# A scratch buffer of its own for each head's maximum in a fused attention and MLP kernel

## The chip, the cores and the metric

The kernel runs on one core of one Trainium2 chip. The metric is the device time of one execution in microseconds (us). Five engines work beside each other, each through its own instructions in order: TensorE (PE; its weight loads are shown as PEld), VectorE (DVE), ScalarE (ACT), GpSimd (POOL) and SyncE (SP), which here issues nearly all DMAs. They wait for each other through semaphores.

## The reference

With x of 2048 rows by 640 columns:

```python
def _A_ref(x, wqkv, wo):                 # H = 32 heads of Dh = 20, window W = 256
    q, k, v = ...                        # x @ wqkv, split into heads
    scores = einsum("bhqd,bhkd->bhqk", q, k) * Dh ** -0.5
    mask = (i - j >= 0) & (i - j < W)
    p = softmax(where(mask, scores, -1e9))
    o = einsum("bhqk,bhkd->bhqd", p, v)
    return o.reshape(B, S, D) @ wo

def _B_ref(x, w1, b1, w2, b2):           # 640 -> 1536 -> 640
    h = relu(x @ w1 + b1) ** 2
    return h @ w2 + b2

xn = layernorm(x)
return x + _A_ref(xn, ...) * silu(_B_ref(xn, ...))
```

All inputs and the output are float32.

## The kernel before

The 2048 rows are 16 blocks of 128. A product that has to be exact is made of three matmuls, with each factor cut into a high and a low part.

A first stage, up to about 113 us, normalizes x, transposes it, and makes v and the first group of q and k. The main stage then runs over steps. A step is one pair of heads (16 pairs) and one block of 128 queries (16 blocks), with some more steps behind, since the later parts of a step lag 13 and 15 steps. The order of every engine's instructions is written out by the program: `tc.manual_schedule` keeps it, and a planner (`due`, `fill`, `clock`) decides at build time how much filling work goes between the parts of a step. One step issues:

- `scores` (L642): for each of the two heads one matmul into a PSUM bank `sps`. Both banks come from the pool `pat`, tag `s`, with two buffers, so the next step's `sps` for the first head takes the bank that the first head's maximum has read, and likewise for the second.
- `scores_t` (L683), for the step 13 back: the transposed scores `stps` of both heads, into one buffer of two banks.
- every 8 steps `max_rows` (L660): the maxima gathered in `mt` are transposed into `stps`, negated, split and stored into two rows of q, so that `stps` comes out with the row's maximum taken off.
- `maxima` (L654): for each of the two heads one VectorE instruction that adds the mask to the scores of up to 384 keys, writes the sum to `junk`, and writes its maximum over the keys into one column of `mt`. Nothing reads `junk`. In the trace one such call is a reduction (CUSTOM_DVE_ANT_0) and the read of its accumulator into `mt` (DVE_READ_ACCUMULATOR2_ANT), both at L658.
- `exps` (L694): the exponential of `stps` into `p` on ScalarE, with two selections on GpSimd for the mask.
- filling work: q and k of the later heads (`qkps`), and the MLP's two products, `hps` (evacuated by ScalarE) and `yps`. `yps` is emptied by an addition on VectorE, `ysb` at L1185, and its bank is then reused. Each filling product is issued in two halves of 64 rows that TensorE works on side by side (L640).
- `values` (L724), once per 8 blocks: a burst of `ops` matmuls that multiplies p by v.

After the last step come the output product `wops` (L800) and its evacuation (L1381).

The weights of the MLP are cut into parts on the way: a copy on ScalarE and a subtraction on VectorE (L991).

A buffer of a pool is taken by its tag. When a tile is taken from a tag whose buffers are all in use, the first instruction that writes it waits until the last use of the tile that had the buffer before. For `junk`, with one buffer for both heads, that last use is the other head's maximum; as both are VectorE's, the wait is one for VectorE's own semaphore.

Of the kernel before, what the change touches and what calls it, by code (L numbers as in the profile page):

```python
# [11 lines left out]
BF16 = mybir.dt.bfloat16  # L12
# [3 lines left out]
P = 128  # L16
# [50 lines left out]
def attn_mlp_kernel(ctx: ExitStack, tc, x, wqkv, wo, w1, b1, w2, b2, out):  # L67
# [516 lines left out]
    at2 = ctx.enter_context(tc.tile_pool(name="at2", bufs=2))  # L584
# [68 lines left out]

    def maxima(p, q, ss, nk):  # L654
        for hh in range(2):
            junk = at2.tile([P, 3 * P], BF16, tag="junk", bufs=1, name="junk")
            m = MG * hh + q % MG
            nc.vector.tensor_tensor_reduce(out=junk[:, :nk], in0=ss[hh][:, :nk], in1=mask[:, 3 * P - nk:], scale=1.0, scalar=-3.0e38, op0=ALU.add, op1=ALU.max, accum_out=mts[q // MG % 2][:, m:m + 1])  # L658

# [756 lines left out]
    with tc.manual_schedule(engines={E_.PE, E_.Activation, E_.DVE, E_.Pool, E_.SP}):  # L1416
# [7 lines left out]
        for s in range(steps):  # L1424
# [29 lines left out]
            if a:  # L1454
                maxima(*a, *sc)
# [51 lines left out]
```

## Time and profile before

| | |
|---|---|
| time, median of 3 runs | 837.44 us (837.16 to 837.87) |
| the profiled execution's own time | 838.13 us |
| its span, first to last instruction | 836.4 us |
| PE busy | 826.2 us (99%) |
| PEld busy | 779.0 us (93%) |
| DVE busy | 477.8 us (57%) |
| ACT busy | 425.5 us (51%) |
| POOL busy | 364.2 us (44%) |
| TensorE's granted clock | 1.000 |

A row of a group reads: line, engine, operation, what it writes and reads with the shapes, how many, then busy time and the mean of one in ns, and the engine's idle time before them with what ended it. A row of the timeline reads: start and duration in us, engine, line, operation, count, and in square brackets how long the engine had been idle before and what released it. A row of the chain in order of time has start, duration and what ran; "issue" there is time in which nothing that the profile shows was waited for, and DVEq is an instruction of VectorE's sequencer, such as a semaphore wait. PE and PEld are two streams of one engine; a matmul's duration contains its way through the array, so that matmuls overlap.

### The profile page before, as it was taken

The page shows a single profiled execution, that of the slowest core. Times are in us where ns is not written, and L with a number is a line of the kernel's source. Part 1 is how long each engine was busy: PE and PEld are TensorE (multiplying, and loading weights), DVE is VectorE, ACT ScalarE, POOL GpSimd, SP SyncE. Part 2 cuts the span into 40 slices and gives each one's busy share as a digit, 9 for nine tenths or more (in the row PEclk, how much of TensorE's full clock was granted, in tenths as well). Part 3 has the DMA queues.
Part 4 walks back from the last instruction along what each step waited for, and adds up shares of the span by engine and source line. Part 5 has one row for each costly group of instructions (what it writes and reads, how often), then busy time and mean ns, then how long its engine had stood idle before and what let it go on. Part 6 is the DMA issues. An engine that isn't in the chain of part 4 may idle for free.

```text
span 836.4 us, 25137 instructions
## 1 busy us (share of the span) xinstructions
PE 826.2 (99%) x10082; PEld 779.0 (93%) x10082; DVE 477.8 (57%) x1398; ACT 425.5 (51%) x760; POOL 364.2 (44%) x672
## 2 busy tenths in 40 slices
PE   8999999999999999999999999999999999999997
PEld 8999999989889999999999989999999999999997
DVE  7855457656578455455455476655455455246763
ACT  6254323545566744744754754844644744664321
POOL 5177900334344542533542543643543643552442
PEclk9999999999999999999999999999999999999999
DMA  6999577878697555546083536585266557346962
GB/s 236 299 390 348 182 215 269 238 260 282 232 324 262 142 173 156 127 157 174 21 268 130 121 108 181 134 244 176 59 222 172 130 177 224 92 131 199 373 251 80
DMA packets 88812, 166.40 MB, mean 199 GB/s; under 512 B 10232, under 2 KB 36472, under 8 KB 87672
## 3 DMA queue, kind: packets, MB, share of 16 engines
q1 hardware_dynamic: 88536, 164.63, 62.7%
q8 instruction: 79, 1.29, 0.7%
q14 instruction: 37, 0.30, 0.1%
q10 hardware_dynamic: 160, 0.16, 0.1%
HBM read 93.66 MB, written 70.52 MB: 196 GB/s over the span
## 4 chain that ended last, share of the span: by engine, by line
PE 94%; DVE 2%; DMA 2%; issue 1%; ACT 1%; SPq 0%; POOL 0%; DVEq 0%; POOLq 0%; ACTq 0%
PE hps L640 20%; PE yps L640 20%; PE qkps L640 13%; PE ops L731 10%; PE wops L800 8%; PE stps L690 5%; PE sps L650 4%; PE vps L239 4%; PE qkps L214 3%; PE vps L362 3%; PE tps L181 1%; DVE junk L658 1%; DMA k_d<-slo 1%; DMA qs<-q_d 1%; PE vps L417 0%
## 5 line engine op out<-in xcount | busy, mean ns | idle before, releaser
L658 DVE CUSTOM_DVE_ANT_0 junk<-sps,mask 128x384 bf16<-128x384 f32 (+2 forms) x512 | 272.4, 532 | 250.9 <-PE sps L650 91.3
L696 ACT ACTIVATE p<-stps 128x768 f32<-128x768 f32 (+2 forms) x256 | 197.5, 772 | 255.5 <-PE stps L690 236.6
L697 POOL TENSOR_SCALAR_AFFINE_SELECT p<-p 128x256 f32<-128x256 f32 x256 | 109.8, 429 | 336.4 <-ACT p L696 334.0
L640 PE MATMUL yps<-w,hh 64*128 64x320 f32 x1536 | 226.1, 309 | 2.2 <-DVE ysb L1185 2.0
L640 PE MATMUL hps<-xb,w 64*128 64x256 f32 (+1 forms) x2100 | 210.0, 304 | 0.0
L640 PEld LDWEIGHTS hps<-xb,w 64*128 64x128 f32 x2100 | 194.7, 186 | 3.5 <-issue 2.7
L640 PEld LDWEIGHTS yps<-w,hh 64*128 64x128 f32 x1536 | 187.9, 185 | 7.3 <-DVE ysb L1185 4.4
L640 PE MATMUL yps<-w,hl 64*128 64x320 f32 x768 | 179.3, 308 | 0.0
L650 PE MATMUL sps<-ks,qs 60*128 60x384 f32 (+2 forms) x512 | 125.4, 335 | 1.0 <-DVE mt L658 1.0
L690 PE MATMUL stps<-qs,ks 62*128 62x384 f32 (+2 forms) x512 | 122.0, 334 | 0.1
L640 PEld LDWEIGHTS yps<-w,hl 64*128 64x128 f32 x768 | 121.4, 185 | 0.4 <-issue 0.4
L640 PE MATMUL qkps<-xT,wgqh 64*128 64x512 f32 x320 | 99.4, 391 | 0.0
L640 PE MATMUL qkps<-xT,wgkh 64*128 64x512 f32 x320 | 98.2, 391 | 0.0
L699 POOL TENSOR_SCALAR_AFFINE_SELECT p<-p 128x256 f32<-128x256 f32 x224 | 95.5, 426 | 0.0
L731 PE MATMUL ops<-p,vp 128*21 128x128 f32 (+1 forms) x2128 | 86.6, 311 | 0.0
L731 PEld LDWEIGHTS ops<-p,vp 128*21 128x21 f32 x2128 | 63.6, 101 | 21.2 <-issue 6.3
L650 PEld LDWEIGHTS sps<-ks,qs 60*128 60x128 f32 x512 | 78.4, 185 | 4.3 <-DVE mt L658 2.2
L690 PEld LDWEIGHTS stps<-qs,ks 62*128 62x128 f32 x512 | 77.5, 187 | 0.7 <-ACT p L696 0.6
L1155 POOL TENSOR_TENSOR hl<-sq,hh 128x512 fp32r<-128x512 f32 x48 | 62.1, 1293 | 16.1 <-ACT sq L1154 15.5
L800 PE MATMUL wops<-wo,oT 128*128 128x320 f32 (+2 forms) x384 | 62.0, 310 | 0.0
L640 PE MATMUL qkps<-xT,wgkl 64*128 64x512 f32 x160 | 61.4, 393 | 0.0
L640 PE MATMUL qkps<-xT,wgql 64*128 64x512 f32 x160 | 61.4, 390 | 0.0
(163 smaller groups left out, 1234.2 us busy)
## 6 DMA issues: line engine op xcount, KB each, us to landing
ks<-k_d SPq DMA_DIRECT2D x64, 240.0 KB
qs<-q_d SPq DMA_DIRECT2D x64, 240.0 KB
xb<-xs SPq DMA_DIRECT2D x60, 256.0 KB
k_d<-shm SPq DMA_DIRECT2D x20, 512.0 KB
q_d<-shm SPq DMA_DIRECT2D x20, 512.0 KB
xs<-xT SPq DMA_DIRECT2D x8, 1280.0 KB
y<-ysb SPq DMA_DIRECT2D x28, 320.0 KB
o<-osb SPq DMA_DIRECT2D x64, 128.0 KB
```

The source lines that it names most:

```text
L214: nc.tensor.matmul(ps, wt[:, c, :], xT[part][b][:, c * BT + t0:c * BT + t0 + n], start=m == 1, stop=m == 3 * KC)
L239: nc.tensor.matmul(ps, xT[xp][b][:, c * BT + t * P: c * BT + (t + 1) * P], wv[wp][:, c, nh * HALF:(nh + 1) * HALF], start=first and m == 0 ...
L640: return nc.tensor.matmul(out, a[r], b_[r], skip_group_check=True, **kw)
L650: nc.tensor.matmul(ss[hh][:, :nk], qs[i][o, q * P:(q + 1) * P], ks[i][o, k0 * P:k0 * P + nk], start=True, stop=True)
L658: nc.vector.tensor_tensor_reduce(out=junk[:, :nk], in0=ss[hh][:, :nk], in1=mask[:, 3 * P - nk:], scale=1.0, scalar=-3.0e38, op0=ALU.add, o ...
L690: nc.tensor.matmul(tps[:, hh, :n], ks[i][o, kb * P:(kb + 1) * P], qs[i][o, kb * P:kb * P + n], start=True, stop=True)
L696: nc.scalar.activation(p32[:, :, :n], tps[:, :, :n], AF.Exp, scale=SCALE)
L697: nc.gpsimd.affine_select(p32[:, :, 0:P], p32[:, :, 0:P], pattern=[[0, 2], [1, P]], compare_op=ALU.is_ge, fill=0.0, base=0, channel_multip ...
L699: nc.gpsimd.affine_select(p32[:, :, 2 * P:], p32[:, :, 2 * P:], pattern=[[0, 2], [-1, P]], compare_op=ALU.is_gt, fill=0.0, base=0, channel ...
L731: nc.tensor.matmul(ot[r0:r0 + VW, c0:c0 + len(part), :], vps[p][:, kb // 4, kb % 4, hh, :], pts[p, kb][:, hh, :].rearrange("p (t n) -> p t ...
L800: nc.tensor.matmul(ps, a, b_, start=j == 0, stop=j == n - 1)
L1155: nc.gpsimd.tensor_sub(hh[1][:, :BT], sq, f32(hh[0]))
```

## The change

`maxima` takes the scratch tile under a tag of its own for each of the two heads, `junk0` and `junk1`, with one buffer each. Everything else is as it was.

```diff
     def maxima(p, q, ss, nk):
         for hh in range(2):
-            junk = at2.tile([P, 3 * P], BF16, tag="junk", bufs=1, name="junk")
+            junk = at2.tile([P, 3 * P], BF16, tag=f"junk{hh}", bufs=1, name="junk")
             m = MG * hh + q % MG
             nc.vector.tensor_tensor_reduce(out=junk[:, :nk], in0=ss[hh][:, :nk], in1=mask[:, 3 * P - nk:], scale=1.0, scalar=-3.0e38, op0=ALU.add, op1=ALU.max, accum_out=mts[q // MG % 2][:, m:m + 1])
```

## The prediction

> **What bounds the kernel now.** I read the page's busy times first, then its chain, then the waits of TensorE's two streams, and then the maxima themselves, line L658, in the source view, the chain in order of time and the timeline.
>
> ```profile
> PE 826.2 (99%) x10082; PEld 779.0 (93%) x10082; DVE 477.8 (57%) x1398; ACT 425.5 (51%) x760; POOL 364.2 (44%) x672
> PE 94%; DVE 2%; DMA 2%; issue 1%; ACT 1%; SPq 0%; POOL 0%; DVEq 0%; POOLq 0%; ACTq 0%
> L658 DVE CUSTOM_DVE_ANT_0 junk<-sps,mask 128x384 bf16<-128x384 f32 (+2 forms) x512 | 272.4, 532 | 250.9 <-PE sps L650 91.3
> ```
>
> TensorE is the bound: busy for 826.2 of 836.4 us and 94% of the chain. VectorE, where the change is, works 57% of the span. A gain on VectorE alone is worth nothing; it counts only where TensorE stands still for VectorE. The waits views of PE and of its weight loads (PEld) name those places (total us, times, longest):
>
> ```profile
> PE yps L640 <- DVE ysb L1185: 2.0, 4, 1.0
> PE sps L650 <- DVE mt L658: 1.0, 2, 0.7
> PEld yps L640 <- DVE ysb L1185: 4.4, 9, 1.3
> PEld sps L650 <- DVE mt L658: 2.2, 5, 1.0
> ```
>
> They are two kinds. The scores matmul of L650 waits until a maximum has read its PSUM bank (mt is what the maximum's second instruction writes). A matmul into yps waits until the addition of L1185 has emptied its bank, and that addition often stands behind a pair of maxima in VectorE's queue. These views leave out waits under about 0.15 us.
>
> Now the pair. Source view of L658, and the chain in order of time at one pair:
>
> ```profile
> L658 DVEq EVENT_SEMAPHORE  x514: 21/21/358, 112.9 to 722.8; - x172
> L658 DVE DVE_READ_ACCUMULATOR2_ANT mt<- x512: 75/83/86, 113.7 to 723.4; 128x1 f32 x171
> ...
> 235.41 0.56 DVE junk L658
> 235.97 0.02 DVE mt L658
> 235.99 0.03 issue
> 236.01 0.02 DVEq L658
> 236.03 0.09 issue
> 236.12 0.11 DVE junk L658
> ```
>
> Each of the 512 maxima is three things: a semaphore wait of VectorE's own queue (x514), the reduction, and the read of the accumulator. The chain passes from the first head's reduction (end 235.97) through its accumulator read, 0.03 us, the semaphore wait of 0.02 us and 0.09 us more to the second head's reduction at 236.12. So the second head waits for the first head's completion: both write the one junk buffer, and nothing else links them.
>
> **The change, part by part.** *Removed:* the second head's wait for the first head of the same step. Its own buffer was last written one step earlier. *Not removed:* the wait instruction itself; each head must still wait for its own buffer's last writer, so I expect some 512 of them, but met already when they are read. No DMA is added, removed or moved, and no queue's order changes.
>
> What one pair gains, from the timeline of VectorE:
>
> ```profile
> 437.19 0.56 DVE L658 CUSTOM_DVE_ANT_0 junk<-sps,mask 128x384 bf16<-128x384 f32 x1 [0.95 <-PE yps L640]
> 437.67 0.08 DVE L658 DVE_READ_ACCUMULATOR2_ANT mt<- 128x1 f32 x1
> 437.90 0.56 DVE L658 CUSTOM_DVE_ANT_0 junk<-sps,mask 128x384 bf16<-128x384 f32 x1
> 438.38 0.08 DVE L658 DVE_READ_ACCUMULATOR2_ANT mt<- 128x1 f32 x1
> 438.38 0.48 DVE L1185 TENSOR_TENSOR ysb<-yps,b2t 128x320 f32<-128x320 f32 x1
> 438.92 0.18 PEld L640 LDWEIGHTS yps<-w,hh 64*128 64x128 f32 x1 [0.26 <-DVE ysb L1185]
> ```
>
> The first accumulator read starts at 437.67 and ends at 437.75; the second head follows at 437.90, 0.23 us after that read's start and 0.15 us after its end. The second accumulator read starts at 438.38, and the addition behind it, which waits for nothing of VectorE's, starts at 438.38 too. Freed of the wait, the second head should behave as this addition does: start at 437.67. A pair is then shorter by 0.23 us. The bounds are 0.15 (it starts only at the read's end) and 0.23; I take 0.23, as the addition is an instruction in the same place. Over 256 pairs that is 59 us of VectorE's time, nearly all of it beside TensorE's work and worth nothing.
>
> The Trainium skill speaks against this ("VectorE: DVE Perf Modes", section "The DRAIN you can't avoid"): the flush after every VectorE instruction cannot be skipped by leaving out semaphores, and a chain of copies took as long with one after each as with one at the end. By that rule the sum would be 0 us. The trace disagrees here: 0.15 us of gap with the wait against none for the addition.
>
> *What TensorE gets back, first kind (additions behind a pair).* In the rows above the weight load at 438.92 stands idle for 0.26 us for the addition, which began when the pair ended. With the pair 0.23 us shorter, the addition ends 0.23 us sooner, and this stall nearly goes. I count 12 such stalls of yps whose addition was held up by a pair with the gap in it, the 9 of the waits view (4.4 us), of which the first and the last stand here, and 3 that are too short for it:
>
> ```profile
> 364.49 0.19 PEld L640 LDWEIGHTS yps<-w,hh 64*128 64x128 f32 x2 [0.30 <-DVE ysb L1185]
> 617.97 0.19 PEld L640 LDWEIGHTS yps<-w,hh 64*128 64x128 f32 x2 [0.21 <-DVE ysb L1185]
> ```
>
> The longer ones give 0.23 each, the three shortest about 0.1: 12 x 0.2 = 2.4 us.
>
> *Second kind (the step after a burst of ops).* One instance, all engines, unrelated rows left out:
>
> ```profile
> 395.30 0.56 DVE L658 CUSTOM_DVE_ANT_0 junk<-sps,mask 128x384 bf16<-128x384 f32 x1 [2.36 <-PE hps L640]
> ...
> 395.68 0.81 ACT L696 ACTIVATE p<-stps 128x768 f32<-128x768 f32 x1 [2.90 <-PE stps L690]
> ...
> 396.01 0.56 DVE L658 CUSTOM_DVE_ANT_0 junk<-sps,mask 128x384 bf16<-128x384 f32 x1
> ...
> 396.49 0.08 DVE L658 DVE_READ_ACCUMULATOR2_ANT mt<- 128x1 f32 x1
> ...
> 396.63 0.18 PEld L650 LDWEIGHTS sps<-ks,qs 60*128 60x128 f32 x1
> 396.63 0.29 PEld L690 LDWEIGHTS stps<-qs,ks 62*128 62x128 f32 x2
> ```
>
> The second head's accumulator read ends at 396.57 and the weight load of the next sps follows at 396.63: TensorE has come round to this bank before it is free. I count 23 such places, the first and the last being:
>
> ```profile
> 186.15 0.08 DVE L658 DVE_READ_ACCUMULATOR2_ANT mt<- 128x1 f32 x1
> ...
> 186.29 0.18 PEld L690 LDWEIGHTS stps<-qs,ks 62*128 62x128 f32 x1
> ...
> 704.65 0.08 DVE L658 DVE_READ_ACCUMULATOR2_ANT mt<- 128x1 f32 x1
> ...
> 704.78 0.18 PEld L650 LDWEIGHTS sps<-ks,qs 60*128 60x128 f32 x1
> ```
>
> What is late next is ScalarE: the exponential at 395.68 ends at 396.49, and stps at 396.63 needs its bank. With the usual 0.06 us behind an end it could start at 396.55, so the place gives 0.08 us, not 0.23: 23 x 0.08 = 1.8 us.
>
> *The rest.* Six or so other sps waits, among them those of the 2.2 us above that a pair feeds, give 0.1 to 0.23: 0.9 us. The longest wait for mt is fed by a first head that TensorE itself released late, and gives nothing:
>
> ```profile
> 320.02 0.18 PEld L650 LDWEIGHTS sps<-ks,qs 60*128 60x128 f32 x1 [0.96 <-DVE mt L658]
> ```
>
> *Sum.* 2.4 + 1.8 + 0.9 = 5.1 us if every stall returns in full. TensorE arriving earlier finds the next bank less ready, and half-idle moments of its two row halves are not all losses; I take three quarters, 3.9 us. Below it lies 0 (all of it handed to ScalarE and the rest), above it 5.1 and a little for stalls too short for me to see. With fixed orders on every engine, ending a wait earlier can't by itself make anything later. The end of the chain is one stretch of TensorE's own, so what is saved before it is kept:
>
> ```profile
> 761.76 70.06 PE wops L800 x475
> ```
>
> *The second buffer* takes 128x384 bf16, 768 bytes of each partition, and moves what its pool places behind it. A tile that comes to lie on another tile of the first stage could wait longer at the handover; the nearest row bounds that:
>
> ```profile
> PEld sps L650 <- DVE vt L384: 0.2, 1, 0.2
> ```
>
> 0.2 us, once, is all that TensorE waits for the first stage now. I take 0 and allow 0.2 either way.
>
> **The rivals.** *(B) The gap closes, but only what idles visibly returns.* If short stalls are filled by the other row half anyway, only PE's own idle time counts: four waits for the addition and one of the two for mt, up to 0.23 us each: about 1.2 us, so 836.2. For it: PE is 99% busy. Against: the weight loads stand idle too, and no later matmul can pass them.
>
> *(C) Nothing happens.* Either the pair stays tied through mt, since both accumulator reads write that tile, or the gap is the price of any two such reductions. Then 837.4. Against the first, two writes into parts of one tile that follow without a gap, two of 0.47 us by their mean in 0.83:
>
> ```profile
> L157 DVE BATCH_NORM_STATS2 st<-xt 128x6 f32<-128x320 f32 x32 | 13.7, 472 | 6.7 <-DMA xt<-in_A_x_dram 6.7
> 17.26 0.83 DVE L157 BATCH_NORM_STATS2 st<-xt 128x6 f32<-128x320 f32 x2
> ```
>
> Against the second stands the addition at 438.38, though it is another instruction; no reduction in this trace goes without the wait. The skill's rule above would give this time as well.
>
> *(D) Slower, through VectorE's subtractions beside GpSimd.* The subtractions of L991 vary:
>
> ```profile
> L991 DVE TENSOR_TENSOR w<-raw,w 128x384 fp32r<-128x384 f32 x28 | 17.9, 654 | 0.0
> 485.47 2.08 DVE L991 TENSOR_TENSOR w<-raw,w 128x384 fp32r<-128x384 f32 x2
> ```
>
> Two in a row took 2.08 us, 1.04 each against the mean of 0.65; I suppose that GpSimd, working on the same memory, holds them up. Pairs that end 0.23 us sooner start such subtractions at other moments of its work; one that lengthens by 0.39 us ahead of an addition stalls TensorE. Three yps stalls have subtractions in the queue; two each would cost 2.3 us, with B's gain 838.5. To end slower by 0.2% (1.67 us) it needs B's 1.2 and 1.7 more, 8 newly slowed ones of the 28. Against: as many may get quicker.
>
> **How the numbers follow.** The profiled execution took 838.13 us, 1.7 over its span of 836.4 and 0.7 above the median of 837.44; the sum is taken from the span and carried over to the median. Forecast (A) 837.44 - 3.9 = 833.5, chance 0.62, own range 831.5 to 835.6; B 0.20 (836.2), C 0.13 (837.4), D 0.05 (838.5). 0.2%, 1.67 us, is about what a measurement tells from no change. A, with a small chance that B's size comes out larger, makes faster 0.68; the rest of B and C make same 0.27; D slower 0.05. The range goes from 831.5, past the full 5.1, to 837.2, which takes in B and the lower part of C.
>
> **What would show it.** The second head starts at the first accumulator read's start or end, 0.48 to 0.57 us behind the first head instead of 0.71. The semaphore waits stay near 512, but lie ahead of the first head's end. Waits of yps for the additions fall from 4.4 us to about 2; after bursts, stps and ScalarE's exponential end the wait in place of mt. VectorE's busy time stays near 478. The prediction is wrong if the 0.71 us stay (C), if they fall while TensorE's waits don't (B), or if subtractions grow (D).

## The result and the profile after

The changed kernel took 832.39 us (median; 832.02 to 832.94) against 837.46 us for the kernel before (837.12 to 838.79): 5.07 us less, a ratio of 0.9938 with the interval [0.9925, 0.9951]. Run once more beside the kernel before on another chip it gave 832.08 against 837.33. The profiled execution took 832.94 us with a span of 831.2.

The page of the changed kernel, busy times and chain, and its group of the maxima:

```profile
PE 822.4 (99%) x10082; PEld 777.8 (94%) x10082; DVE 456.6 (55%) x1398; ACT 425.2 (51%) x760; POOL 361.6 (43%) x672
PE 97%; DVE 1%; ACT 1%; DMA 0%; issue 0%; ACTq 0%
L658 DVE CUSTOM_DVE_ANT_0 junk<-sps,mask 128x384 bf16<-128x384 f32 (+2 forms) x512 | 252.1, 530 | 257.1 <-PE sps L650 107.9
```

TensorE's share of the chain went from 94% to 97%: what was taken out lay between its matmuls. VectorE's busy time fell by 21.2 us, though one reduction takes nearly as long as before, 530 ns in the mean against 532. The busy time counts moments in which two instructions run only once, and now something overlaps, as the timeline of VectorE shows, at the place whose rows the prediction has at 437.19 to 438.92:

```profile
434.96 0.56 DVE L658 CUSTOM_DVE_ANT_0 junk<-sps,mask 128x384 bf16<-128x384 f32 x1 [1.18 <-PE yps L640]
435.44 0.08 DVE L658 DVE_READ_ACCUMULATOR2_ANT mt<- 128x1 f32 x1
435.44 0.55 DVE L658 CUSTOM_DVE_ANT_0 junk<-sps,mask 128x384 bf16<-128x384 f32 x1
435.92 0.08 DVE L658 DVE_READ_ACCUMULATOR2_ANT mt<- 128x1 f32 x1
435.92 0.48 DVE L1185 TENSOR_TENSOR ysb<-yps,b2t 128x320 f32<-128x320 f32 x1
...
436.46 0.18 PEld L640 LDWEIGHTS yps<-w,hl 64*128 64x128 f32 x1
```

The second head starts at 435.44, with the first head's accumulator read, 0.48 us behind the first head instead of 0.71. The first head's row lasts to 435.52, so the two reductions of a pair overlap by 0.08 us. The 512 reductions last 512 x 0.530 = 271.4 us and fill 252.1: 19.3 of the 21.2 us are this overlap. The accumulator reads have no part in it; before, too, a read lay inside the row of its own reduction (437.67 to 437.75, in 437.19 to 437.75). The addition starts 0.96 us after the pair's start instead of 1.19, and the weight loads for yps behind it no longer carry the idle 0.26 us. The next pair's first head before and after, from the same two timelines:

```profile
439.83 0.56 DVE L658 CUSTOM_DVE_ANT_0 junk<-sps,mask 128x384 bf16<-128x384 f32 x1 [0.96 <-PE sps L650]
```

```profile
437.37 0.56 DVE L658 CUSTOM_DVE_ANT_0 junk<-sps,mask 128x384 bf16<-128x384 f32 x1 [0.96 <-PE sps L650]
```

From the pair's first head to the next pair's it was 439.83 - 437.19 = 2.64 us and is 437.37 - 434.96 = 2.41: TensorE got the full 0.23 us at this place.

The waits views of PE and PEld, and the semaphore waits at L658:

```profile
PE yps L640 <- DVE ysb L1185: 1.2, 2, 1.0
PE stps L690 <- ACT p L696: 0.2, 1, 0.2
PEld yps L640 <- DVE ysb L1185: 1.9, 3, 1.3
PEld sps L650 <- DVE mt L658: 0.2, 1, 0.2
L658 DVEq EVENT_SEMAPHORE  x25: 21/21/358, 113.2 to 687.9; - x25
```

Weight loads that waited for an addition fell from 4.4 us to 1.9, those for a maximum from 2.2 to 0.2. Of 514 semaphore waits at L658, 25 are left.

The step after a burst of ops, where the prediction has rows from 395.30 to 396.63, now reads:

```profile
393.43 0.56 DVE L658 CUSTOM_DVE_ANT_0 junk<-sps,mask 128x384 bf16<-128x384 f32 x1 [2.59 <-PE hps L640]
...
393.81 0.81 ACT L696 ACTIVATE p<-stps 128x768 f32<-128x768 f32 x1 [2.89 <-PE stps L690]
...
394.39 0.08 DVE L658 DVE_READ_ACCUMULATOR2_ANT mt<- 128x1 f32 x1
...
394.67 0.18 PEld L690 LDWEIGHTS stps<-qs,ks 62*128 62x128 f32 x1
```

The second head's read ends at 394.47, and nothing waits for it. The weight load of stps at 394.67 follows the exponential, which ends at 394.62. It comes 1.24 us after the pair's start, where it came 1.33 us after.

### The profile page after: what moved, and what is told of

Same layout as the page of the kernel before. It is cut to its first block, busy times and chain, and to the rows that moved or that the text cites. A ratio compares the mean times of both kernels' runs of the same rounds, so it can differ in the third digit from the quotient of the medians.

```text
span 831.2 us, 24648 instructions
## 1 busy us (share of the span) xinstructions
PE 822.4 (99%) x10082; PEld 777.8 (94%) x10082; DVE 456.6 (55%) x1398; ACT 425.2 (51%) x760; POOL 361.6 (43%) x672
## 4 chain that ended last, share of the span: by engine, by line
PE 97%; DVE 1%; ACT 1%; DMA 0%; issue 0%; ACTq 0%
PE yps L640 21%; PE hps L640 20%; PE qkps L640 14%; PE ops L731 10%; PE wops L800 9%; PE stps L690 5%; PE sps L650 5%; PE vps L239 4%; PE qkps L214 3%; PE vps L362 3%; PE tps L181 1%; DVE w L991 0%; PE vps L417 0%; PE vps L407 0%; DMA xt<-in_A_x_dram 0%
## 5 line engine op out<-in xcount | busy, mean ns | idle before, releaser
L658 DVE CUSTOM_DVE_ANT_0 junk<-sps,mask 128x384 bf16<-128x384 f32 (+2 forms) x512 | 252.1, 530 | 257.1 <-PE sps L650 107.9
L697 POOL TENSOR_SCALAR_AFFINE_SELECT p<-p 128x256 f32<-128x256 f32 x256 | 107.7, 421 | 332.9 <-ACT p L696 331.4
L640 PEld LDWEIGHTS yps<-w,hh 64*128 64x128 f32 x1536 | 185.8, 185 | 4.8 <-issue 2.3
L640 PE MATMUL yps<-w,hl 64*128 64x320 f32 x768 | 175.5, 308 | 0.0
L650 PE MATMUL sps<-ks,qs 60*128 60x384 f32 (+2 forms) x512 | 129.0, 333 | 0.0
L690 PE MATMUL stps<-qs,ks 62*128 62x384 f32 (+2 forms) x512 | 126.8, 331 | 0.2 <-ACT p L696 0.2
L640 PEld LDWEIGHTS yps<-w,hl 64*128 64x128 f32 x768 | 117.7, 185 | 0.4 <-issue 0.4
L699 POOL TENSOR_SCALAR_AFFINE_SELECT p<-p 128x256 f32<-128x256 f32 x224 | 95.4, 426 | 0.0
L690 PEld LDWEIGHTS stps<-qs,ks 62*128 62x128 f32 x512 | 81.6, 187 | 1.2 <-ACT p L696 0.6
L650 PEld LDWEIGHTS sps<-ks,qs 60*128 60x128 f32 x512 | 80.8, 185 | 1.9 <-issue 0.3
```

Of the source, the lines that this page charges most:

```text
L640: return nc.tensor.matmul(out, a[r], b_[r], skip_group_check=True, **kw)
L650: nc.tensor.matmul(ss[hh][:, :nk], qs[i][o, q * P:(q + 1) * P], ks[i][o, k0 * P:k0 * P + nk], start=True, stop=True)
L690: nc.tensor.matmul(tps[:, hh, :n], ks[i][o, kb * P:(kb + 1) * P], qs[i][o, kb * P:kb * P + n], start=True, stop=True)
L697: nc.gpsimd.affine_select(p32[:, :, 0:P], p32[:, :, 0:P], pattern=[[0, 2], [1, P]], compare_op=ALU.is_ge, fill=0.0, base=0, channel_multip ...
L699: nc.gpsimd.affine_select(p32[:, :, 2 * P:], p32[:, :, 2 * P:], pattern=[[0, 2], [-1, P]], compare_op=ALU.is_gt, fill=0.0, base=0, channel ...
```

## The experiments

Three theories could give 5 us. *W*: the second head no longer waits for the first inside a pair, and what TensorE loses at known places comes back. *L*: everything placed behind the scratch buffer moved by 768 bytes. *Q*: 489 semaphore waits left VectorE's queue, on both heads, and that alone makes it quicker.

**A wide shared buffer** keeps the wait and moves the tiles:

```diff
-            junk = at2.tile([P, 3 * P], BF16, tag="junk", bufs=1, name="junk")
+            junk = at2.tile([P, 6 * P], BF16, tag="junk", bufs=1, name="junk")
```

> One buffer for both heads as before, but 6*P wide, so that everything placed behind it lies where the change puts it. Theory W (the second head's wait inside a pair): the wait stays, so 837.4 us, within 0.2%; the two heads stay 0.71 us apart. Theory L (the gain comes from where the tiles lie): 832.4 us.

Measured: 837.21 us against 837.34, ratio 1.0003 [0.9994, 1.0012]. The place of the tiles brings nothing; L falls.

**One tile with a half for each head** takes the wait inside the pair away and keeps the one on the step before:

```diff
+        both_junk = at2.tile([P, 2, 3 * P], BF16, tag="junk", bufs=1, name="junk")
         for hh in range(2):
-            junk = at2.tile([P, 3 * P], BF16, tag="junk", bufs=1, name="junk")
+            junk = both_junk[:, hh, :]
```

> One tile per step with a half for each head: the second head has nothing to wait for inside the pair, the first head still waits for the step before. Theory W: about 832.4 us, as with the change, some 256 semaphore waits at L658, heads 0.48 us apart. Theory Q (the gain comes from the semaphore waits that disappeared from VectorE's queue, 489 of 514, so of both heads alike): about half, near 835.

Measured: 832.04 us against 837.34, ratio 0.9939 [0.9927, 0.9952]: all of the gain, with half of the semaphore waits left. Source view (the line is L659 here) and timeline:

```profile
L659 DVEq EVENT_SEMAPHORE  x258: 21/21/358, 114.2 to 715.2; - x129
...
394.19 0.56 DVE L659 CUSTOM_DVE_ANT_0 junk<-sps,mask 128x384 bf16<-128x384 f32 x1 [2.59 <-PE hps L640]
394.67 0.08 DVE L659 DVE_READ_ACCUMULATOR2_ANT mt<- 128x1 f32 x1
394.67 0.55 DVE L659 CUSTOM_DVE_ANT_0 junk<-sps,mask 128x384 bf16<-128x384 f32 x1
```

**Buffers by step** does the opposite:

```diff
-            junk = at2.tile([P, 3 * P], BF16, tag="junk", bufs=1, name="junk")
+            junk = at2.tile([P, 3 * P], BF16, tag=f"junk{q % 2}", bufs=1, name="junk")
```

> Two buffers, used by even and odd query blocks; both heads of a step share one. The wait inside the pair stays, the one on the step before goes. Theory W: 837.4 us, within 0.2%, 256 semaphore waits, heads 0.71 us apart. Theory Q: about half of the gain, near 835.

Measured: 836.94 us against 837.34, ratio 0.9997 [0.9988, 1.0006]: no difference, though as many waits went.

```profile
L658 DVEq EVENT_SEMAPHORE  x259: 21/21/358, 112.8 to 722.0; - x130
...
394.60 0.56 DVE L658 CUSTOM_DVE_ANT_0 junk<-sps,mask 128x384 bf16<-128x384 f32 x1 [2.35 <-PE hps L640]
395.08 0.08 DVE L658 DVE_READ_ACCUMULATOR2_ANT mt<- 128x1 f32 x1
395.31 0.56 DVE L658 CUSTOM_DVE_ANT_0 junk<-sps,mask 128x384 bf16<-128x384 f32 x1
```

These two kernels have the same number of semaphore waits within one and differ by 4.9 us. What counts is which head waits: the second 0.00 us behind the start of the accumulator read in the one, 0.23 in the other. Q falls, W stands.

**Only after bursts, and everywhere else.** Next, where the gain lies. First, own buffers in the 32 pairs right after a burst:

```diff
-            junk = at2.tile([P, 3 * P], BF16, tag="junk", bufs=1, name="junk")
+            junk = at2.tile([P, 3 * P], BF16, tag=f"junk{hh if q % 8 == 7 else 0}", bufs=1, name="junk")
```

> A buffer for each head only at the steps right after a burst of ops (query blocks 7 and 15), one shared buffer elsewhere: 32 of 256 pairs. Theory W with the prediction's terms: 1.8 us less than before, 835.6. If every pair counts alike (59 us of VectorE's time shortened evenly): an eighth of 5.1, 836.8. If ScalarE's exponential takes all of it over: 837.4.

Measured: 835.54 us against 837.34, ratio 0.9980 [0.9971, 0.9990]: 1.8 us, from an eighth of the pairs. Some of it belongs to the first kind of stall: two of the additions stand behind a pair that follows a burst. The stall of one of them in the weight loads of the kernel before:

```profile
377.67 0.18 PEld L640 LDWEIGHTS yps<-w,hh 64*128 64x128 f32 x1 [0.40 <-DVE ysb L1185]
```

and in this kernel, with VectorE's rows ahead of it:

```profile
375.00 0.56 DVE L658 CUSTOM_DVE_ANT_0 junk<-sps,mask 128x384 bf16<-128x384 f32 x1 [2.59 <-PE yps L640]
375.48 0.08 DVE L658 DVE_READ_ACCUMULATOR2_ANT mt<- 128x1 f32 x1
375.48 0.55 DVE L658 CUSTOM_DVE_ANT_0 junk<-sps,mask 128x384 bf16<-128x384 f32 x1
375.96 0.08 DVE L658 DVE_READ_ACCUMULATOR2_ANT mt<- 128x1 f32 x1
375.96 0.49 DVE L1185 TENSOR_TENSOR ysb<-yps,b2t 128x320 f32<-128x320 f32 x1
...
376.50 0.18 PEld L640 LDWEIGHTS yps<-w,hh 64*128 64x128 f32 x1 [0.17 <-DVE ysb L1185]
```

The stall shrank from 0.40 to 0.17 us, by 0.23. The other, 0.72 us at 495.33 in the kernel before, is 0.48 us here, at 493.74. Then the counterpart:

```diff
+            junk = at2.tile([P, 3 * P], BF16, tag=f"junk{hh if q % 8 != 7 else 0}", bufs=1, name="junk")
```

> The counterpart of the kernel with own buffers only after bursts: own buffers at all other steps (224 of 256 pairs), one shared buffer at query blocks 7 and 15. That kernel gave 1.8 us. If the terms add up and no stall that is ended comes back elsewhere: 5.1 to 5.3 less 1.8, so 3.4 us, 833.9. If stalls come back (the prediction's three quarters): the two parts alone give more than both together, so under 833.3.

Measured: 834.03 us against 837.22, ratio 0.9964 [0.9951, 0.9976]: 3.2 us. The two parts, 1.8 and 3.2, make 5.0, and both together gave 5.1 and 5.3. They add up. The times alone leave room for something else: the interval of this run reaches down to 0.9951, 833.1 us, just below the 833.3 set for stalls that come back. The traces are clearer. By the source views, the time from the start of the first maximum to that of the last was 608.5 us with the wide shared buffer, 606.6 and 605.1 with the two parts, and 603.6 and 603.2 in the two traces of the change: 1.9 and 3.4 us against 4.9 and 5.3. And the two additions behind a burst hold the weight loads up by 0.17 and 0.48 us in the change (at 375.80 and 492.57), just as with buffers only after bursts.

**Late pairs only:**

```diff
+            junk = at2.tile([P, 3 * P], BF16, tag=f"junk{hh if q % 8 != 7 and p >= 5 else 0}", bufs=1, name="junk")
```

> Own buffers only from the sixth pair of heads on, and not at query blocks 7 and 15: the stage in which yps is emptied by VectorE. By the prediction's terms: 10 of the 12 waits of yps for an addition lie here behind such a pair, 2.0 us, and some 0.3 of other waits, so 835.0. If every pair counts alike (154 of 256 pairs): 834.2.

Measured: 834.89 us against 837.22, ratio 0.9975 [0.9966, 0.9984]: 2.3 us, the prediction's figure for these waits. The even count (834.2) is 0.7 us off, less than the interval's half width of 0.75, so against the even count the eighth of pairs above speaks more clearly.

**What is left: the subtractions.** In the changed kernel the two longest waits for an addition remain. The longest, in VectorE's timeline and in that of the weight loads:

```profile
482.71 2.32 DVE L991 TENSOR_TENSOR w<-raw,w 128x384 fp32r<-128x384 f32 x2
484.95 0.48 DVE L1185 TENSOR_TENSOR ysb<-yps,b2t 128x320 f32<-128x320 f32 x1
...
485.48 0.18 PEld L640 LDWEIGHTS yps<-w,hh 64*128 64x128 f32 x1 [1.26 <-DVE ysb L1185]
```

The addition stands behind two subtractions. The change was given these on GpSimd:

```diff
-                nc.vector.tensor_sub(lin1(t_, olo + c0, c1 - c0), raw[:, c0:c1], f32(lin1(t_, ohi + c0, c1 - c0)))
+                nc.gpsimd.tensor_sub(lin1(t_, olo + c0, c1 - c0), raw[:, c0:c1], f32(lin1(t_, ohi + c0, c1 - c0)))
```

> The change, and the MLP weights' 48 subtractions of L991 on GpSimd instead of VectorE. With the change, the longest waits of yps for an addition (1.3 and 0.5 us) are those whose addition stands behind subtractions. Theory: they go, and the time falls by up to 1.7 us to 830.7. Rival: GpSimd's queue delays its selections and the hl of the MLP, and TensorE waits for these instead: 832.4 or more.

and, apart from that, planned further apart:

```diff
-            later(1.9 + 0.7 * k, go)
+            later(1.9 + 1.4 * k, go)
```

> The change, and the subtractions of L991 planned 1.4 us apart instead of 0.7, so that fewer stand in a row ahead of an addition. Theory: the two long waits shrink by half, 831.5. Rival: they only move in front of other additions: 832.4, within 0.2%.

Measured: 832.07 and 831.99 us against 837.22 for the kernel before. The waits views of PEld and PE with the subtractions on GpSimd:

```profile
PEld sps L650 <- DVE mt L658: 0.8, 3, 0.3
PEld yps L640 <- DVE ysb L1185: 0.2, 1, 0.2
PE stps L690 <- DMA qs<-mrow: 0.5, 1, 0.5
```

The waits for additions fell from 1.9 to 0.2 us, as the theory had it, but waits for a maximum rose from 0.2 to 0.8, and one of 0.5 us for a DMA appeared. Of the 1.7 us hoped for, 0.3 at most came. With the subtractions further apart:

```profile
PEld yps L640 <- DVE ysb L1185: 1.2, 3, 0.6
```

The longest wait was halved, from 1.3 to 0.6 us, as the theory had it, but the 0.4 us that the time lies lower are no more than the runs of the change itself vary. The change and this version were then run together on one chip:

> The change itself, on one chip with the version below, as its reference: 832.4 us.

> The change with L991 on GpSimd once more, beside the change on the same chip. If the 0.3 us seen between them on two chips hold: 832.1 against 832.4; a difference this small is within what a run varies, so anything from 831.7 to 832.7 is no difference.

Measured: 832.08 us (831.86 to 832.27) and 831.85 us (831.31 to 832.43). The two overlap; no version here beats the change by more than the runs vary.

## Why the prediction was right, and where its size was off

*The pair.* Right to the row. It took 0.23 us from the addition at 438.38 that starts with the accumulator read; the second head now does that. The lower bound, 0.15, didn't come true. The rule of the Trainium skill that was weighed against it ("VectorE: DVE Perf Modes", "The DRAIN you can't avoid"), by which leaving a semaphore out saves nothing, isn't borne out for these instructions: 0.23 us a pair with the wait, 0.00 without. The same section says that a next instruction that isn't held starts earlier, which the prediction left out and which the trace bears out. Rival C is gone in both its forms; writing two columns of mt doesn't tie the heads.

*First kind of stall* (12 x 0.2 = 2.4 us). The places shown gave 0.23 each, and the runs with late pairs, which hold 10 of the 12 and 0.3 us of others, gave 2.3 against 2.3. That agreement is partly luck, as two errors offset each other. Stalls too short for the waits view gave more than 0.1: at the weight load of 692.14, the time from the pair's first head to the next pair's was 692.92 - 690.41 = 2.51 us before and 687.87 - 685.60 = 2.27 after. And one of the 12 gave nothing: the stall of 1.26 us before and after. Its two subtractions took 2.08 us in the trace before and 2.32 after, so VectorE lost there the 0.24 us that the pair had gained. GpSimd's `hl` runs beside them, before and after:

```profile
485.16 1.30 POOL L1155 TENSOR_TENSOR hl<-sq,hh 128x512 fp32r<-128x512 f32 x1 [2.10 <-ACT sq L1154]
487.47 0.48 DVE L1185 TENSOR_TENSOR ysb<-yps,b2t 128x320 f32<-128x320 f32 x1
```

```profile
482.63 1.30 POOL L1155 TENSOR_TENSOR hl<-sq,hh 128x512 fp32r<-128x512 f32 x1 [2.10 <-ACT sq L1154]
```

The addition behind the subtractions starts 1.01 us after the end of `hl` before (486.46) and 1.02 us after it in the change (483.93): the subtractions start earlier beside `hl` and end no earlier. That fits rival D's mechanism, here for 0.24 us; no run moves `hl` alone, so its part isn't shown.

*Second kind* (23 x 0.08 = 1.8 us). The reading was right: the exponential is late next, and the one place shown gave 1.33 - 1.24 = 0.09 us. The run with buffers only after bursts gave the predicted 1.8, but part of that belongs to the first kind, 0.23 and 0.24 at its two additions. At most 1.3 us are left for the 23 places, so the term was too large by some 0.5.

*The sum.* The full sum was 5.1 us, measured were 5.07 and 5.25. The step that failed is the factor of three quarters: TensorE arriving earlier was to find the next bank less ready. It didn't, since the two parts of the change add up to the whole. That the full sum comes so close is in part luck: with the second kind too large, the other terms must have given about as much more, which is shown only at the one short stall above. In this kernel a pair starts when TensorE has made its scores, so an earlier TensorE moves the next pair by the same amount. Rival B, which let only PE's visible idle time return (1.2 us), fails for the same reason: weight loads that idle for 0.1 to 0.3 us cost time although PE counts as busy.

*Side claims.* The prediction kept some 512 semaphore waits; 25 are left. With a buffer for each head, or with buffers by step, the built program leaves out the waits for an earlier step. What decides that isn't shown. An instruction of VectorE between two writes isn't enough: in the kernel before an addition often stands between two pairs, and all 512 waits are there. That the waits for an earlier step went brought nothing, since they were met anyway. It also kept VectorE's busy time near 478 us; it forgot that an overlap is counted once.

*The longest stall.* The wait of 0.96 us at 320.0, put down at zero, differs from execution to execution. It is absent with the wide shared buffer, which keeps every wait. The load of sps ahead of it in the trace before, and the same stretch of weight loads with the wide buffer:

```profile
318.75 0.18 PEld L650 LDWEIGHTS sps<-ks,qs 60*128 60x128 f32 x1
```

```profile
318.82 0.18 PEld L650 LDWEIGHTS sps<-ks,qs 60*128 60x128 f32 x1
318.96 0.18 PEld L640 LDWEIGHTS yps<-w,hh 64*128 64x128 f32 x1
319.29 0.18 PEld L650 LDWEIGHTS sps<-ks,qs 60*128 60x128 f32 x1
```

Between the two loads of sps lie 0.47 us with the wide buffer, and 1.27 us (318.75 to 320.02) in the first trace. The 0.80 us between the two are about the 0.7 us by which the profiled execution before stood above its median. A load of queries that landed late would explain it. At the same place in the kernel with late pairs only, the matmul waits for one:

```profile
319.43 0.41 PE L650 MATMUL sps<-ks,qs 60*128 60x384 f32 x1 [0.28 <-DMA qs<-q_d]
```

In the trace before, no view names such a load, so the cause there isn't shown.

## What to carry to other kernels

A scratch output that nobody reads is still a buffer, and two neighbouring instructions that share it wait for each other; give neighbours different ones, or two halves of one. Price such a wait not by the engine's time (59 us here) but by the places where the bounding engine stands behind that engine, and look there for who is late next. When several stalls are ended whose next start hangs on the bounding engine itself, they can add up in full, as the 1.8 and 3.2 us did here. It is no rule: of the 1.7 us of waits that went with the subtractions on GpSimd, 0.3 at most came off the time.

## What the runs showed of the hardware

A VectorE reduction with an accumulator read behind it can have the next reduction start at the start of that read, 0.48 us after a 0.56 us reduction began; a wait for the first one's completion puts it 0.23 us later. A semaphore wait that is already met costs VectorE nothing that the time shows: with 259 of them and with 514 the time was 836.94 and 837.21 us on the chip of the first four experiments.
